# Normalization pairs: the meeting of two half sums moved from VectorE to ScalarE and GpSimd, and the inner factors of the second Strassen level formed in two pieces

## The chip, the cores and the metric

The kernel runs on one core of a Trainium2 chip. A time is the device time of one execution in microseconds (us), and where several runs are given their median is used. A core has TensorE (PE, the matrix engine), VectorE (DVE), ScalarE (ACT), GpSimd (POOL) and the queues that start transfers (DMA); each engine works through its own list of instructions in order, and semaphores make one wait for another. A profiled execution gives start and length of every instruction; its span is the time from the first to the last of them.

## The reference, cut to what matters

```python
batch, n_heads, seq, head_dim = (8, 12, 448, 64)

def rmsnorm(x, g):
    rms = np.sqrt(np.mean(x * x, axis=-1, keepdims=True) + 1e-06)
    return x / rms * g
q_n, k_n = (rmsnorm(q, g_q), rmsnorm(k, g_k))
scores = scale * np.matmul(q_n, k_n.transpose(0, 1, 3, 2))
attn = softmax(scores)
attn_out = np.matmul(attn, v)            # (8, 12, 448, 64) -> x of (8*448, 768)

h = x @ w_in                             # 3584 x 768 x 2048
g = h - np.tanh(h)
out = g @ w_out                          # 3584 x 2048 x 768
```

(The softmax is written out in the reference, with the maximum subtracted; its line is shortened here.) So there are 96 heads of attention with a normalization of every row of q and k, and then a two-layer network over 3584 tokens. The two weights come as float64.

## The kernel before

**Pairs and slots.** The heads are taken in pairs: eight batches of six pairs make 48 steps `s`. The attention of step `s` and the preparation of the following steps are spread over one slot; between the parts of a slot, `run(ns)` lets the network's matmuls of an earlier batch go on for a given amount of work. The network is a generator (`mlp`) which yields the estimated time of each matmul. So nothing is scheduled on the chip: the order of each engine's list is written out by the Python program, in the order in which the slot and the generator call the instructions.

**A slot.** `slot(s)` (from step 12 on) begins with the scores of the next step's last chunk of keys (the `p_last` tiles), and then with `visit`, a run of 128 small matmuls that takes the values of step `s` and the scores of step `s + 1` together. The scores use three PSUM banks in turn; ScalarE's exponentials (line 570) release them. After the visit come fourteen work points, with a share of the network's matmuls ahead of each. Among them are: the sums of the exponentials for step `s + 1` on VectorE (lines 595, 601, 608, then 705 and 712), ScalarE's gathering copies (720), VectorE's scaling and transposes of step `s + 2` (528, 538, 542), ScalarE's squares for step `s + 3` (499), and the normalization of `s + 3`.

**The norm of a pair.** From step 15 on q and k of a pair lie "by blocks": partitions hold four groups of 32 (two heads, two halves of the 64 elements), so a row's sum of squares is in two halves on two groups of partitions. `norm_blocks` (line 506) reduces each half into `rr_mine` (128 x 28). `meet_blocks` (514, 515) adds, group by group, the own half and the partner's into `rr_other`, and scales it and adds the epsilon. `power_blocks` (521) raises it to the power -1/2 on GpSimd, at the start of the next slot. `scale_blocks` (528) multiplies q and k by it.

**The network.** Its products are done by a fast scheme with seven products for a 2 x 2 split, in the order 1, 5, 6, 2, 3, 7, 4 (`ORDER`), with sums of blocks ahead of them. For the first layer (`hidden`, matmuls on line 831) and for the second layer of batches 0 and 1 there is one level. From batch 2 on, two batches form a pair, and their second layer (`project_pair`, matmuls on line 1082) has two levels: seven outer products over (batch, half), each with seven inner products. Two outer products run after the first batch's hidden layer and five after the second's. `outer_sum` (1032, VectorE) forms the outer sums in place; `inner_sum` (1040, GpSimd) forms the four sums `u` of an outer product, each of 128 x 896, in four rotating buffers. Of the inner products, 5, 6, 7 and 4 read the sums 0, 1, 2 and 3. The three `mm` PSUM banks go round: product 3 is added on top of product 5's bank once VectorE has read product 5 (line 1089), and 2 and 7 likewise on top of 1 and 6. The activation of the hidden layer is ScalarE's tanh (878) and a subtraction on GpSimd or VectorE (879), with two `th` buffers; a third tanh waits until the first subtraction has released its buffer. GpSimd also makes the first-level sums of the attention's output (787).

Of the kernel before, what the change touches and what calls it, by code (L numbers as in the profile page):

```python
# [13 lines left out]
ALU = mybir.AluOpType  # L14
# [130 lines left out]
def bounded_path(tc, ctx, q, k, v, moe_w_in, moe_w_out, out, g_col, ident, ones, half_ones, neg_half, early):  # L145
# [17 lines left out]
    nc = tc.nc  # L163
    B, H, S, D = q.shape
# [17 lines left out]
    BL = 32  # L182
# [252 lines left out]
    normed, turned, probs, sums, whole, xT, tt = {}, {}, {}, {}, {}, {}, {}  # L435
# [73 lines left out]
    def meet_blocks(s):  # L509

        mine, other = normed["rr", s]
        for g in range(P // BL):
            own, met = slice(g * BL, (g + 1) * BL), slice((g ^ 1) * BL, ((g ^ 1) + 1) * BL)
            nc.vector.tensor_tensor(out=other[own], in0=mine[own], in1=mine[met], op=ALU.add)  # L514
        nc.vector.tensor_scalar(out=other, in0=other, scalar1=1.0 / D, scalar2=1e-6, op0=ALU.mult, op1=ALU.add)  # L515
        normed["rr", s] = other

    def power_blocks(s):

        mine = normed["rr", s]  # L520
        nc.gpsimd.tensor_tensor(  # L521
            out=mine, in0=mine, in1=neg_half[:, :1].to_broadcast([P, 2 * NJ]), op=ALU.pow
        )
# [26 lines left out]
    def scores(s, c, apart=False):  # L550

        rr, kT, qT = turned[s]
        n = S if c < KF else HS
        name, bufs = ("p", 2) if c < 2 else ("p_full", 1) if c < KF else ("p_last", 2)
        if c == 1:
            p = probs[s, 1] = probs[s, 0]
        else:
            p = probs[s, c] = pp.tile([P, 2, 2 if c < 2 else 1, n], F32, name=name, bufs=bufs)
        tiles = [sc_bank() for _ in range(2)]

        def score(h, i):
            at, first = (i * BL, 0) if c < KF else (i * BL % KR, i * BL // KR * n)
            r = slice(h * D, (h + 1) * D)
            nc.tensor.matmul(  # L564
                tiles[h][i * BL : (i + 1) * BL, :n], lhsT=kT[r, c * P + at : c * P + at + BL],
                rhs=qT[r, first : first + n], start=True, stop=True,
            )

        def exp(h):
            nc.scalar.activation(  # L570
                p[:, h, c if c < 2 else 0, :], tiles[h][:, :n], AF.Exp,
                scale=1.0 if rr is None else rr[:, 0, 2 * c + h : 2 * c + h + 1],
            )

        if apart:
            return [(lambda i, h=h: score(h, i), lambda h=h: exp(h)) for h in range(2)]
        for i in range(P // BL):
            for h in range(2):
                score(h, i)
        for h in range(2):  # L580
            exp(h)
# [28 lines left out]
    def last_values(s, av):  # L610

        v_nat, p = loaded["v", s], probs[s, KF]
        for n in range(2):
            keys, at = slice(n * KR, (n + 1) * KR), n * HS if s >= FOLDED else 0
            for m in range(2):
                for h in range(2):
                    r = (2 * m + h) * BL
                    nc.tensor.matmul(  # L618
                        av[n][r : r + BL, at : at + HS], lhsT=v_nat[keys, h, KF, m * BL : (m + 1) * BL],
                        rhs=p[keys, h, 0], start=(s < FOLDED), stop=False, skip_group_check=(s >= FOLDED),  # L620
                    )
# [54 lines left out]
    def totals(s, dn):  # L676

        parts = [t[:, h, n * HS : (n + 1) * HS] for t in sums.get(s, ()) for n in range(2) for h in range(2)]
        parts = [(parts, [ones[:, :BL]] * 2)] if parts else []
        if not sums.pop(s):  # L680
            for p in full(s):
                parts.append(
                    ([p[:, h, n * HS : (n + 1) * HS] for n in range(2) for h in range(2)], [ones[:, :BL]] * 2)
                )
            last = probs[s, KF]
            parts.append(([last[:, h, 0] for _ in range(2) for h in range(2)], [half_ones[:, n] for n in range(2)]))
        for i, (moving, by) in enumerate(parts):
            for n in range(2):
                for h in range(2):
                    r = (2 * n + h) * BL  # L690
                    nc.tensor.matmul(
                        dn[r : r + BL, :HS], lhsT=by[n], rhs=moving[2 * n + h],
                        start=(i == 0), stop=(i == len(parts) - 1),
                    )
        rs = whole[s] = sp.tile([P, HS], F32, name="rs")
        nc.vector.reciprocal(rs, dn[:, :HS])
# [34 lines left out]
    def widen_sums(s):  # L731

        total = whole[s]
        wide = whole[s] = late["blocks"].tile([2 * BL, NJ, BL], F32, name="sum_w")
        nc.scalar.copy(out=wide, in_=total[:, :, None].to_broadcast([2 * BL, NJ, BL]))

    def turn_sums(s):

        wide = whole[s]
        rs = whole[s] = late["blocks"].tile([2 * BL, S], F32, name="rs_T")  # L740
        nc.vector.transpose(out=rs, in_=wide.rearrange("p j k -> p (j k)"))
# [273 lines left out]
    KB = HF // 2  # L1015

    def rows(p, f, n, cols):
        which, half = HOME[p]
        return late["pair_g"][which][:, half * HF + f : half * HF + f + n, cols]
# [14 lines left out]
    def inner_sum(p, i):  # L1034

        us = late["us"]
        x11, x12, x21, x22 = (rows(p, f, KB, cols) for f in (0, KB) for cols in (slice(0, HS), slice(HS, S)))
        u = us[p, i] = late["pair"].tile([P, KB, HS], F32, name="u", bufs=4)
        a, z = ((x12, x11), (x22, us.get((p, 0))), (x22, x12), (x21, us.get((p, 1))))[i]
        nc.gpsimd.tensor_tensor(out=u, in0=a, in1=z, op=ALU.subtract)  # L1040

    def beside_hidden(b, j, p):

# [258 lines left out]
    def gap_ns(s):  # L1302

        if s < 2 * NP:
            return H_NS / 12 if s % NP < 3 else 4 * S / ENGINE_NS * CD * CF / 12
        if s < 3 * NP:
            return (H_NS + O_NS + AHEAD_NS) / (4 * NP)
        n = (s - 3 * NP) % (2 * NP)
        return (H_NS / 16, OUTER_NS * SOON / 8, H_NS / 16, OUTER_NS * (len(OUTER) - SOON) / 8)[(n > 3) + (n > 5) + (n > 9)]

    def has(s):
        return 0 <= s < NS
# [69 lines left out]
    def slot(s):  # L1382

        gap = gap_ns(s)
        av = av_banks
        if has(s + 1):
            scores(s + 1, KF)
        if s < FOLDED:
            last_values(s, av)
            totals(s, sc_bank())  # L1390
            divide(s, values(s, av))
            for c in range(KF):
                scores(s + 1, c)
        else:
            visit(s, av)
        if has(s + 2):
            load(s + 2, "v")
        rows, ahead, following = has(s + 2), has(s + 3), has(s + 1)
        folded = following and s + 1 >= FOLDED
        first = s + 3 == TURNED  # L1400
        scaled = rows and not first
        if scaled:
            power_blocks(s + 2)
        work = (
            (
                (following, lambda: add(s + 1, False)), (first, lambda: turn(s + 2, sc_bank(), sc_bank())),
                (ahead and not first, lambda: load_blocks(s + 3)),
            ),
            (
                (following, lambda: add_third(s + 1)), (first, lambda: load_blocks(s + 3)),  # L1410
                (True, lambda: x_sums_later(s, 0)),
            ),
            ((following, lambda: add_last(s + 1)),),
            ((folded, lambda: fold(s + 1)),),
            ((folded, lambda: fold_rest(s + 1)), (True, lambda: x_sums_later(s, 1))),
            ((scaled, lambda: scale_blocks(s + 2)),),
            ((scaled, lambda: turn_blocks(s + 2, 0)),),
            ((folded, lambda: gather(s + 1, 0)), (scaled, lambda: turn_blocks(s + 2, 1))),
            ((folded, lambda: gather(s + 1, 1)), (ahead, lambda: square_blocks(s + 3))),
            ((folded, lambda: spread_sums(s + 1)), (True, lambda: x_sums_later(s, 2))),  # L1420
            ((ahead, lambda: norm_blocks(s + 3)),),
            ((folded, lambda: widen_sums(s + 1)), (ahead, lambda: meet_blocks(s + 3))),
            ((folded, lambda: turn_sums(s + 1)),),
            (),
        )
        for point in work:
            run(4 * gap / (len(work) + 1))
            for wanted, fn in point:
                if wanted:
                    fn()  # L1430
        run(4 * gap / (len(work) + 1))
# [358 lines left out]
```

## Time and profile before

| | |
|---|---|
| time, median of 3 runs | 1406.79 us (1406.57 to 1408.85) |
| profiled execution: time, span | 1407.51 us, 1405.4 us |
| PE busy | 1341.7 us, 95% of the span |
| DVE busy | 1077.7 us, 77% |
| POOL busy | 727.2 us, 52% |
| ACT busy | 523.3 us, 37% |
| mean granted TensorE clock | 0.985 |
| DVE meets: 132 additions (514) and 33 scalings (515) | 80.2 and 17.9 us busy |
| POOL powers (521), 33 | 166.8 us |
| POOL inner sums (1040), 84 | 195.8 us in all |

In a group's row the columns are: line, engine, operation, tiles written and read, shapes, count, then busy time and mean length of one in ns, then the idle time of the engine just before these instructions, with what ended most of it. In a list of waits the numbers are the total, how often, and the longest, in us. In a timeline the columns are start (us from the span's start), length, engine, line, operation, tiles and count, with idle time before it in brackets.

### The profile page before, as it was taken

How to read it: one execution, taken by the hardware profiler on the slowest of the kernel's cores; microseconds unless marked ns; L12 is line 12 of the kernel's file. 1: busy time of each engine (PE TensorE's matmuls, PEld its weight loads, DVE VectorE, ACT ScalarE, POOL GpSimd, SP SyncE). 2: the span in 40 equal slices, each digit the busy share in tenths (PEclk: the TensorE clock that was granted, in tenths of full speed). 3: DMA queues.
4: the chain of work that ended last, by engine and by line, in shares of the span. 5: the costliest groups of instructions: out<-in, count | busy, mean ns of one | idle time of the engine just before them, and what ended most of it. 6: DMA issues, size and time to landing. Idle time of an engine off the chain costs nothing.

```text
span 1405.4 us, 29010 instructions
## 1 busy us (share of the span) xinstructions
PE 1341.7 (95%) x11336; PEld 1048.9 (75%) x11336; DVE 1077.7 (77%) x1558; ACT 523.3 (37%) x1194; POOL 727.2 (52%) x409
## 2 busy tenths in 40 slices
PE   7988999999999998999999999999999999899996
PEld 3467854488889885788768787678876788689884
DVE  4999989669857888789988688879997688533563
ACT  7856554343332533343321434253511244311100
POOL 4756666156762439335784336733597234712661
PEclk9999999999999999999999999999999999999998
DMA  7879889889998665475545866375644775355544
GB/s 173 187 208 252 267 240 243 254 230 329 328 267 238 162 178 124 92 200 156 130 128 143 190 173 166 89 173 155 165 120 126 154 199 151 102 155 171 168 150 80
DMA packets 371686, 253.52 MB, mean 180 GB/s; under 512 B 282196, under 2 KB 310228, under 8 KB 371540
## 3 DMA queue, kind: packets, MB, share of 16 engines
q1 hardware_dynamic: 371536, 251.57, 66.4%
q8 instruction: 92, 1.51, 0.4%
q14 instruction: 54, 0.44, 0.1%
q10 hardware_dynamic: 4, 0.00, 0.0%
HBM read 205.23 MB, written 46.27 MB: 179 GB/s over the span
## 4 chain that ended last, share of the span: by engine, by line
PE 71%; DVE 17%; DMA 4%; issue 3%; SPq 2%; ACT 1%; POOL 1%; ACTq 0%; DVEq 0%; POOLq 0%
PE mm L831 34%; PE mm L1082 17%; PE sc L564 8%; PE mm L1246 5%; PE sc L630 5%; DVE rr_other L514 2%; DVE rows L608 2%; DMA w_f<-w_in 1%; DMA gT<-in_moe_w_in_dram 1%; DVE acc L1089 1%; PE sc L668 1%; DVE g L1032 1%; DVE xT L756 1%; PE sc L618 1%; DVE rows L601 1%
## 5 line engine op out<-in xcount | busy, mean ns | idle before, releaser
L831 PE MATMUL mm<-xT,w_f 128*128 128x224 f32 x1296 | 264.3, 353 | 1.7 <-DVE s L902 1.7
L831 PEld LDWEIGHTS mm<-xT,w_f 128*128 128x128 f32 x1296 | 244.4, 190 | 8.2 <-issue 4.3
L564 PE MATMUL sc<-qT,kT 64*32 64x448 f32 (+1 forms) x3072 | 217.8, 500 | 4.3 <-ACT p_last L570 3.1
L831 PE MATMUL mm<-tt,w_f 128*128 128x224 f32 x1044 | 213.3, 355 | 0.4
L521 POOL TENSOR_TENSOR rr_other<-rr_other,neg_half 128x28 f32<-128x28 f32 x33 | 166.8, 5056 | 83.8 <-DVE rr_other L515 83.2
L831 PEld LDWEIGHTS mm<-tt,w_f 128*128 128x128 f32 x1044 | 195.2, 190 | 17.7 <-issue 15.4
L879 POOL TENSOR_TENSOR gT<-s,th 128x448 f32<-128x448 f32 x60 | 73.3, 1236 | 201.3 <-ACT th L878 199.4
L1082 PE MATMUL mm<-gT,w_f 128*128 128x224 f32 (+1 forms) x480 | 138.6, 443 | 13.7 <-DVE acc L1089 12.6
L1082 PE MATMUL mm<-u,w_f 128*128 128x224 f32 x672 | 139.8, 360 | 1.3 <-DVE acc L1089 1.3
L1082 PEld LDWEIGHTS mm<-u,w_f 128*128 128x128 f32 x672 | 130.0, 195 | 8.6 <-issue 4.5
L1082 PEld LDWEIGHTS mm<-gT,w_f 128*128 128x128 f32 x480 | 92.9, 196 | 53.7 <-issue 36.2
L564 PEld LDWEIGHTS sc<-qT,kT 64*32 64x32 f32 x3072 | 73.1, 106 | 76.3 <-issue 45.6
L879 POOL TENSOR_TENSOR g<-s,th 128x448 f32<-128x448 f32 x36 | 43.3, 1216 | 165.8 <-ACT th L878 150.4
L630 PE MATMUL sc<-p,v_nat 64*32 64x448 f32 x1120 | 119.4, 537 | 0.0
L1082 PE MATMUL mm<-g,w_f 128*128 128x224 f32 (+1 forms) x360 | 104.2, 443 | 11.5 <-DVE s L1089 6.9
L1082 PEld LDWEIGHTS mm<-g,w_f 128*128 128x128 f32 x360 | 70.4, 197 | 39.8 <-issue 26.0
L720 ACT COPY sum_g<-sum 32x14 f32<-32x14 f32 x280 | 56.3, 201 | 112.9 <-DVE sum L712 107.2
L752 DVE TENSOR_TENSOR xT<-xT,sc 128x448 f32<-128x448 f32 x32 | 19.7, 617 | 101.2 <-PE sc L564 58.5
L570 ACT ACTIVATE p<-sc 128x448 f32<-128x448 f32 x132 | 72.0, 546 | 40.4 <-PE sc L564 35.9
L514 DVE TENSOR_TENSOR rr_other<-rr_mine 32x28 f32<-32x28 f32 x132 | 80.2, 607 | 3.8
L1246 PE MATMUL mm<-gT,w_out 128*128 128x448 f32 x192 | 74.3, 542 | 0.0
L878 ACT ACTIVATE th<-s 128x448 f32<-128x448 f32 x96 | 53.1, 571 | 54.4 <-DVE s L910 16.7
(187 smaller groups left out, 2429.0 us busy)
## 6 DMA issues: line engine op xcount, KB each, us to landing
w_f<-w_in SPq DMA_DIRECT2D x196, 384.0 KB, 3.5
w_f<-w_inner SPq DMA_DIRECT2D x63, 512.0 KB, 3.6
w_f<-w_out SPq DMA_DIRECT2D x42, 512.0 KB, 3.9
w_raw<-in_moe_w_out_dram SPq DMA_DIRECT2D x16, 768.0 KB, 5.3
w_in<-w_out SPq DMA_DIRECT2D x21, 384.0 KB, 5.5
qk_nat<-in_q_dram SPq DMA_DIRECT2D x132, 56.0 KB, 2.6
qk_nat<-in_k_dram SPq DMA_DIRECT2D x132, 56.0 KB, 2.5
g<-w_out SPq DMA_DIRECT2D x14, 512.0 KB, 5.4
```

What stands on the lines that cost most here:

```text
L514: nc.vector.tensor_tensor(out=other[own], in0=mine[own], in1=mine[met], op=ALU.add)
L521: nc.gpsimd.tensor_tensor(out=mine, in0=mine, in1=neg_half[:, :1].to_broadcast([P, 2 * NJ]), op=ALU.pow)
L564: nc.tensor.matmul(tiles[h][i * BL : (i + 1) * BL, :n], lhsT=kT[r, c * P + at : c * P + at + BL], rhs=qT[r, first : first + n], start=True ...
L570: nc.scalar.activation(p[:, h, c if c < 2 else 0, :], tiles[h][:, :n], AF.Exp, scale=1.0 if rr is None else rr[:, 0, 2 * c + h : 2 * c + h ...
L608: nc.vector.tensor_tensor(out=part, in0=part, in1=last[n * KR : (n + 1) * KR], op=ALU.add)
L630: nc.tensor.matmul(av[g][i * BL : (i + 1) * BL, :S], lhsT=v_nat[keys, h, c, m * BL : (m + 1) * BL], rhs=p[keys, h], start=first, stop=True ...
L720: nc.scalar.copy(out=acc[h * BL : (h + 1) * BL, g], in_=part[g * BL : (g + 1) * BL, h * NJ : (h + 1) * NJ])
L831: nc.tensor.matmul(bank[:, f * HS : (f + 1) * HS], lhsT=w[:, c * width + f, :], rhs=moving[p](c), start=(first and f == 0 and c == 0), sto ...
L878: nc.scalar.activation(th, h, AF.Tanh, bias=0.0, scale=1.0)
L879: eng.tensor_tensor(out=g[:, rows, cols], in0=h, in1=th, op=ALU.subtract)
L1082: nc.tensor.matmul(bank[:, :n], lhsT=w(i), rhs=mv, start=(first and i == 0), stop=(i == len(moving) - 1), skip_group_check=not first,)
L1246: nc.tensor.matmul(bank[:, :S], lhsT=w_out_row(f, n // HC)[:, n % HC * P : (n % HC + 1) * P], rhs=g[:, f, :], start=(f == 0), stop=(f == C ...
```

## The change

Two edits. First, ScalarE copies the partner's half (`rr_mine` of the neighbouring group of 32 partitions) into `rr_other`, four copies of 32 x 28, one work point later than VectorE's additions were; GpSimd then adds `rr_other` to `rr_mine`, scales and adds the epsilon, and raises to the power, all at the start of the next slot. VectorE no longer takes part. Second, every inner sum `u` is made by two GpSimd instructions of 128 x 448 in place of one of 128 x 896.

```diff
         mine, other = normed["rr", s]
         for g in range(P // BL):
-            own, met = slice(g * BL, (g + 1) * BL), slice((g ^ 1) * BL, ((g ^ 1) + 1) * BL)
-            nc.vector.tensor_tensor(out=other[own], in0=mine[own], in1=mine[met], op=ALU.add)
-        nc.vector.tensor_scalar(out=other, in0=other, scalar1=1.0 / D, scalar2=1e-6, op0=ALU.mult, op1=ALU.add)
-        normed["rr", s] = other
+            nc.scalar.copy(out=other[g * BL : (g + 1) * BL], in_=mine[(g ^ 1) * BL : ((g ^ 1) + 1) * BL])
 
     def power_blocks(s):
 
-        mine = normed["rr", s]
+        mine, other = normed["rr", s]
+        nc.gpsimd.tensor_tensor(out=mine, in0=mine, in1=other, op=ALU.add)
+        nc.gpsimd.tensor_scalar(out=mine, in0=mine, scalar1=1.0 / D, scalar2=1e-6, op0=ALU.mult, op1=ALU.add)
+        normed["rr", s] = mine
         nc.gpsimd.tensor_tensor(
             out=mine, in0=mine, in1=neg_half[:, :1].to_broadcast([P, 2 * NJ]), op=ALU.pow
         )
@@
         a, z = ((x12, x11), (x22, us.get((p, 0))), (x22, x12), (x21, us.get((p, 1))))[i]
-        nc.gpsimd.tensor_tensor(out=u, in0=a, in1=z, op=ALU.subtract)
+        for half in (slice(0, KB // 2), slice(KB // 2, KB)):
+            nc.gpsimd.tensor_tensor(out=u[:, half], in0=a[:, half], in1=z[:, half], op=ALU.subtract)
@@
             ((ahead, lambda: norm_blocks(s + 3)),),
-            ((folded, lambda: widen_sums(s + 1)), (ahead, lambda: meet_blocks(s + 3))),
-            ((folded, lambda: turn_sums(s + 1)),),
+            ((folded, lambda: widen_sums(s + 1)),),
+            ((folded, lambda: turn_sums(s + 1)), (ahead, lambda: meet_blocks(s + 3))),
             (),
```

## The prediction

> **What bounds the kernel now.** The first part of the page and the shares of the chain came first:
>
> ```profile
> PE 1341.7 (95%) x11336; PEld 1048.9 (75%) x11336; DVE 1077.7 (77%) x1558; ACT 523.3 (37%) x1194; POOL 727.2 (52%) x409
> PE 71%; DVE 17%; DMA 4%; issue 3%; SPq 2%; ACT 1%; POOL 1%; ACTq 0%; DVEq 0%; POOLq 0%
> ```
>
> PE sets the time and is idle for 1405.4 - 1341.7 = 63.7 us. Removing VectorE work pays only where PE idles for VectorE, so next came the list of PE's waits, with the groups that the change touches:
>
> ```profile
> PE mm L1082 <- DVE acc L1089: 18.6, 10, 2.7
> PE mm L1082 <- DVE s L1089: 8.0, 4, 3.5
> L514 DVE TENSOR_TENSOR rr_other<-rr_mine 32x28 f32<-32x28 f32 x132 | 80.2, 607 | 3.8
> L720 ACT COPY sum_g<-sum 32x14 f32<-32x14 f32 x280 | 56.3, 201 | 112.9 <-DVE sum L712 107.2
> ```
>
> 26.6 us of idle, 14 waits, all in the two-level second layer, where product 3, 7 or the block behind product 4 needs a bank that VectorE has not read yet. The timelines around the first such wait (VectorE, GpSimd, TensorE) say why it is late:
>
> ```profile
> 529.52 7.33 DVE L514 TENSOR_TENSOR rr_other<-rr_mine 32x28 f32<-32x28 f32 x4
> 536.89 1.05 DVE L515 TENSOR_SCALAR rr_other<-rr_other 128x28 f32<-128x28 f32 x1
> ...
> 530.59 2.12 POOL L1040 TENSOR_TENSOR u<-gT,u 128x896 f32<-128x896 f32 x1
> 532.66 2.12 POOL L1040 TENSOR_TENSOR u<-gT 128x896 f32<-128x896 f32 x1
> 534.73 2.08 POOL L1040 TENSOR_TENSOR u<-gT,u 128x896 f32<-128x896 f32 x1
> ...
> 536.36 1.68 PE L1082 MATMUL mm<-gT,w_f 128*128 128x224 f32 x8
> 540.77 3.33 PE L1082 MATMUL mm<-gT,w_f 128*128 128x224 f32 x8 [2.73 <-DVE acc L1089]
> ```
>
> A meet addition (median 182 ns on line 514) takes 2.05 us when an inner sum is in flight: each waits for one GpSimd instruction to end. Five instructions worth 0.9 us hold VectorE from 529.5 to 537.9, and the read of product 5 comes at 540.32. And behind the gap eight matmuls take 3.33 us, not 1.68: the granted clock was 0.50 in 540.6 to 543.9. I find eight such stretches of 3.41 us behind the waits of this stage. At full use each costs 3.41 x 0.5 = 1.7 us more.
>
> [...] The trace has the 3.41 us stretches, but gaps of 2.2 us bring them; the one of 2.06 us at 884.00 did not. [...]
>
> **The change part by part.** *VectorE loses* 132 additions and 33 scalings, 80.2 + 17.9 = 98 us busy. Its order is otherwise the same. *GpSimd gains* an addition and a scaling of 128 x 28 in front of each power. No row shows them; the subtraction takes 1.13 us at 448 elements (line 879) and 2.07 at 896, so about 0.19 + 2.1 ns x 28 = 0.25 us each, an estimate; bounds 0.1 and 0.65 (the 224-element form of line 787). I take 0.5 us a slot, 17 us in all. *Halved sums:* 2 x 1.13 = 2.26 for 2.07, 0.2 us each, 84 x 0.2 = 17 us of GpSimd. It cuts a VectorE wait from up to 2.05 to up to 1.1 us, and each half has its own wait on PE, so a product can begin 1.1 us ahead of the second half. *ScalarE gains* four copies at a pitch of 0.225 us (line 720: 201 ns), 0.9 us a slot, now in front of the next slot's `p_last`.
>
> *Gain, stage by stage.* (1) Waits at 538.03 (2.73), 547.12 (2.22) and in the second pair at 874.88 (2.63), 884.00 (2.06). Without the meets VectorE is free at 529.5 and waits for ScalarE's xT (534.8, 535.2 with the copies). Line 752 takes 0.6, the two of 756 up to 1.15 each beside half sums, so product 5 is read at 538.1, where PE needs it at 538.03: some 0.1 is left. The chain behind it (595, 601, two of 608, 705) then falls under the power, which does not block VectorE (756, 595 and 601 had their usual 0.6 and 1.1 us beside it), so 608 takes 0.6 and not 2.4, and the block's bank is read at 543.4 for a need at 543.0: 0.4 is left. Saved 2.6 + 1.8 and 2.5 + 1.7 = 8.6, and three half-clock stretches, 5.1.
> (2) At 721.20 and 1056.29 (3.44, 3.46) the meets stand directly in front of the read that PE wants:
>
> ```profile
> 718.92 3.40 DVE L514 TENSOR_TENSOR rr_other<-rr_mine 32x28 f32<-32x28 f32 x4
> 722.35 1.94 DVE L515 TENSOR_SCALAR rr_other<-rr_other 128x28 f32<-128x28 f32 x1
> 724.20 0.68 DVE L1089 TENSOR_TENSOR s<-mm,s 128x224 f32<-128x224 f32 x2
> ```
>
> Both go whole, with their stretches: 6.9 + 3.4 = 10.3.
> (3) At 683.73 and 1018.81 (2.3 each) the wait goes too, but GpSimd is late next:
>
> ```profile
> 682.29 6.09 POOL L521 TENSOR_TENSOR rr_other<-rr_other,neg_half 128x28 f32<-128x28 f32 x1
> 688.35 2.07 POOL L1040 TENSOR_TENSOR u<-g,u 128x896 f32<-128x896 f32 x1
> ...
> 687.99 4.54 PE L1082 MATMUL mm<-u,w_f 128*128 128x224 f32 x16
> ```
>
> Product 4 (the second eight, from 690.85) reads the sum that ends at 690.42. That sum stands behind the power, and now behind two halved sums (0.4) and the two new instructions (0.5). PE would arrive about 687.5 and wait to about 690. I take 0.8 saved each, 1.6, instead of 4.0 each.
> (4) 1209 to 1219, where there are no meets any more (gaps 0.32, 1.08, 2.65): 595 and 601 take 2.6 us beside whole sums; halves save about 1.7 of the gaps, and the stretch stays.
> (5) 642.96 and 978.20 (0.9, 0.8): a 608 of 2.4 us beside a sum; 1.5 saved.
> Sum 8.6 + 5.1 + 10.3 + 1.6 + 1.7 + 1.5 = 28.8.
>
> *Loss: ScalarE in front of p_last.* ScalarE before the visit at 506.86:
>
> ```profile
> 507.47 0.55 ACT L735 COPY sum_w<-sum_all 64x448 f32<-64x448 f32 x1
> 508.37 0.58 ACT L878 ACTIVATE th<-s 128x448 f32<-128x448 f32 x1 [0.36 <-POOL gT L879]
> 508.86 0.51 ACT L898 COPY s<-mm 128x448 f32<-128x448 f32 x1
> 509.27 0.61 ACT L570 ACTIVATE p_last<-sc 128x224 f32<-128x224 f32 x2
> ```
>
> Visits last 5.43 us where `p_last` starts up to 1.3 us after their start, and 6.37 where it starts 2.41 after: what is beyond 1.47 us is lost, since the second wave of scores needs the bank. Already 10 us go so. The copies come behind `sum_w` (the reduction 506 has ended at 507.75): 508.03 to 508.93. 0.36 of it falls into the wait for GpSimd, so the third tanh, the copy 898 and `p_last` come 0.57 later. I did this for all 33 slots: 9 lose about 0.58 (5.2), 6 whose `p_last` is now at 1.13 to 1.19 lose 0.22 to 0.29 (1.5), five others 0.5 in all, 13 nothing, as ScalarE idles there. Sum 7.2; 1.3 of it lies in the slots of (3) and vanishes in the wait for GpSimd: 5.9.
>
> Net -28.8 + 5.9 = -22.9. The profiled execution took 1407.51 (span 1405.4 and 2.1 around it), 0.7 over the median, so 1384.6 for it and 1384 as median. The halved sums' and small instructions' 34 us of GpSimd cost nothing elsewhere, as GpSimd is half idle and the sums of the other products are ready 4 to 20 us ahead; where that cover fails is (3).
>
> **Rivals.** *GpSimd takes the place everywhere.* VectorE's chain re-forms behind half sums (756, 595, 601 at 1.1 us of wait each) and the power, pushed back, no longer covers 608. Then half of (1) is left, 6.9, with (2) 10.3 and (5) 1.5, less 7.2: -11.5, 1395. For it: GpSimd works without a break from 682 to 724. *All of it.* Copies fit into ScalarE's pauses, the half sums let product 4 begin in time, and the gaps of (4) and their stretch go: 28.8 + 6.4 + 4 - 1 = -38, 1369. *Slower: the copies hold up every visit.* If `p_last` slips by the whole 0.9 us in all 33 slots, 29.7 us are lost; the eleven visits that stall already would idle about 2 us, and two half-clock stretches add 3.4. Against 28.8 of gain: +4, 1411. It decides from 28.8/33 = 0.87 us a slot. Against it: in 13 slots ScalarE waits for PE anyway. *The halves do nothing,* since two back-to-back halves keep VectorE out as one does: (4), (5) and a third of (1) go, about 1391; between the cases.
>
> **How the numbers follow.** Forecast, with its own range 1376 to 1392: 0.50. GpSimd in its place or halves without effect, 1391 to 1401: 0.22. All of it: 0.12. Slower: 0.13. About no change (the gaps move on): 0.03. Cutting half of the lowest and most of the slower case leaves 1369 to 1404. A measurement of this kernel tells 0.2% (2.8 us) from no change; the chances are 0.84 faster, 0.03 within, 0.13 slower.
>
> **What would show it.** After: PE idle about 45 us, its waits for line 1089 under 8 us, at most four half-clock stretches after 500 us, new waits of the second layer for `u` of 2 to 3 us near 685 and 1015; 168 half sums of 1.1 to 1.3 us; `p_last` 0.5 us later in the hidden stage, its visits up to 7.0 us. It is wrong if visits of 5.43 us become rare, if the new GpSimd instructions take over 0.65 us, or if reads of product 5 stay late.

## The result, and the profile after

The changed kernel takes 1390.59 us, the median of four runs (1390.16 to 1391.89); the kernel before, run beside it, 1407.47. The ratio is 0.9882 (95% interval 0.987 to 0.9895): 16.9 us less. The span of the profiled execution fell from 1405.4 to 1388.4 us. The forecast was 1384 with a range of 1376 to 1392, so the gain is 6 us smaller than the 22.9 worked out.

The first part of the page after, and the shares of its chain of waits:

```profile
PE 1335.9 (96%) x11336; PEld 1046.3 (75%) x11336; DVE 963.2 (69%) x1393; ACT 550.9 (40%) x1326; POOL 766.1 (55%) x559
PE 75%; DVE 9%; DMA 4%; ACT 4%; POOL 3%; SPq 3%; issue 2%; ACTq 0%; DVEq 0%; POOLq 0%
```

VectorE's share of the chain falls from 17% to 9%, and ScalarE's and GpSimd's grow from 1% each to 4 and 3. PE is idle for 1388.4 - 1335.9 = 52.5 us, 11.2 less than before; the other 5.8 us come from its own busy time, which goes with three stretches at half clock behind 500 us instead of eight (the one at the very end, which both have, apart). The list of PE's waits shows who took VectorE's place (lines below 1040 are the same in both kernels, those after it are one higher now):

```profile
PE mm L1083 <- POOL u L1041: 6.9, 2, 3.5
PE sc L564 <- ACT p_last L570: 6.3, 12, 1.0
PE mm L1083 <- DVE acc L1090: 5.2, 7, 2.6
```

Late reads by VectorE, 26.6 us in 14 waits before, are down to 5.2 in 7. In front stand two waits that did not exist, for an inner sum of GpSimd, and twelve in which the scores of a visit wait for ScalarE's `p_last` (before, three of 3.1 us in all). What the new instructions take, from the one-line views of ScalarE's copies and GpSimd's addition (count, then least, median and longest in ns):

```profile
L513 ACT COPY rr_other<-rr_mine x132: 209/213/216, 301.6 to 1165.6; 32x28 f32<-32x28 f32 x132
L518 POOL TENSOR_TENSOR rr_mine<-rr_mine,rr_other x33: 237/243/1092, 304.7 to 1167.5; 128x28 f32<-128x28 f32 x33
```

A copy takes what the forecast took from line 720, and the addition 0.24 us where nothing holds it up, against an estimate of 0.25; six of the 33 were held up, the longest to 1.09 us.

Both kernels issue the same 11336 matmuls in the same order. So I compare the start of the k-th matmul in both traces and read off how much each stage of the forecast gained or lost (times of the kernel before; us; negative is a gain):

| stage | forecast | measured |
|---|---|---|
| (1) 528 to 566 and 865 to 895 | -13.7 | -12.1 |
| (2) 715 to 740 and 1050 to 1075 | -10.3 | -10.6 |
| (3) 673 to 715 and 1008 to 1050 | -1.6 | +5.6 |
| (4) 1195 to 1225 | -1.7 | -2.2 |
| the rest: visits, (5) | +4.4 | +2.4 |
| sum | -22.9 | -16.9 |

One row differs: (3). The others are off by 2 us at most.

**Where it went as worked out.** VectorE's timeline in stage (1):

```profile
535.71 2.50 DVE L756 TENSOR_TENSOR xT<-xT,rs_T 64x448 f32<-64x448 f32 x2
538.23 0.39 DVE L1090 TENSOR_TENSOR acc<-mm,s 128x224 f32<-128x224 f32 x1
...
541.52 1.27 DVE L608 TENSOR_TENSOR rows<-rows,p_last 64x448 f32<-64x448 f32 x2
...
543.86 0.35 DVE L1090 TENSOR_TENSOR acc<-mm,acc 128x224 f32<-128x224 f32 x1
```

The reads come at 538.23 and 543.86, where 538.1 and 543.4 were forecast. The gaps of 2.73 and 2.22 us shrink to 0.42 and 0.41. Line 608 lies under the power, and two of them take 1.27 us instead of up to 2.4 each.

**Where it did not.** GpSimd's timeline in the first half of stage (3), before the change and after it, and below them PE's after:

```profile
676.90 2.13 POOL L1040 TENSOR_TENSOR u<-g,u 128x896 f32<-128x896 f32 x1
...
680.09 2.08 POOL L1040 TENSOR_TENSOR u<-g 128x896 f32<-128x896 f32 x1
```

```profile
670.39 3.10 POOL L1041 TENSOR_TENSOR u<-g,u 128x448 f32<-128x448 f32 x2
...
674.54 2.61 POOL L1041 TENSOR_TENSOR u<-g 128x448 f32<-128x448 f32 x2
677.11 0.62 POOL L518 TENSOR_TENSOR rr_mine<-rr_mine,rr_other 128x28 f32<-128x28 f32 x1
677.82 0.21 POOL L519 TENSOR_SCALAR rr_mine<-rr_mine 128x28 f32<-128x28 f32 x1
678.12 5.60 POOL L521 TENSOR_TENSOR rr_mine<-rr_mine,neg_half 128x28 f32<-128x28 f32 x1
683.69 2.21 POOL L1041 TENSOR_TENSOR u<-g,u 128x448 f32<-128x448 f32 x2
```

```profile
679.73 1.68 PE L1083 MATMUL mm<-u,w_f 128*128 128x224 f32 x8
684.86 3.36 PE L1083 MATMUL mm<-u,w_f 128*128 128x224 f32 x8 [3.46 <-POOL u L1041]
```

PE is done with product 7 at 681.40 and stands for 3.46 us, until the first half of product 4's sum is ready at 684.8. Then eight matmuls take 3.36 us instead of 1.68: the granted clock is 0.50 from 684.9 to 690.4. The same happens in the second pair (3.46 us of wait, half clock from 1014.7 to 1018.2).

I count from the end of the second subtraction 879 (676.82 before, 670.43 after), which starts GpSimd's work here in both kernels. Before, the power ended 11.6 us later and product 4 began 14.0 us later. After, the power ends 13.3 us later and product 4 begins 14.4 us later, although its first half is enough now. The second pair gives the same 14.0 and 14.4.

### The profile page after: what moved, and what is told of

It reads as the page before. It is cut to its first block, busy times and chain, and to the rows that moved or that the text cites. A ratio compares the mean times of both kernels' runs of the same rounds, so it can differ in the third digit from the quotient of the medians.

```text
span 1388.4 us, 29145 instructions
## 1 busy us (share of the span) xinstructions
PE 1335.9 (96%) x11336; PEld 1046.3 (75%) x11336; DVE 963.2 (69%) x1393; ACT 550.9 (40%) x1326; POOL 766.1 (55%) x559
## 3 DMA queue, kind: packets, MB, share of 16 engines
q8 instruction: 92, 1.51, 0.4%
## 4 chain that ended last, share of the span: by engine, by line
PE 75%; DVE 9%; DMA 4%; ACT 4%; POOL 3%; SPq 3%; issue 2%; ACTq 0%; DVEq 0%; POOLq 0%
PE mm L831 33%; PE mm L1083 22%; PE sc L564 8%; PE mm L1247 5%; PE sc L630 4%; DMA w_f<-w_in 2%; DVE xT L756 1%; PE sc L668 1%; DMA w_raw<-in_moe_w_in_dram 1%; POOL u L1041 1%; DVE rows L608 1%; ACT th L878 1%; PE sc L618 1%; SPq L125 1%; SPq L287 1%
## 5 line engine op out<-in xcount | busy, mean ns | idle before, releaser
L564 PE MATMUL sc<-qT,kT 64*32 64x448 f32 (+1 forms) x3072 | 220.6, 500 | 7.5 <-ACT p_last L570 6.3
L521 POOL TENSOR_TENSOR rr_mine<-rr_mine,neg_half 128x28 f32<-128x28 f32 x33 | 163.8, 4963 | 2.7
L1083 PE MATMUL mm<-gT,w_f 128*128 128x224 f32 (+1 forms) x480 | 133.0, 429 | 5.2 <-DVE acc L1090 5.0
L630 PE MATMUL sc<-p,v_nat 64*32 64x448 f32 x1120 | 122.5, 537 | 0.0
L1041 POOL TENSOR_TENSOR u<-gT 128x448 f32<-128x448 f32 x48 | 65.5, 1385 | 15.6 <-PE mm L1083 15.5
L878 ACT ACTIVATE th<-mm 128x448 f32<-128x448 f32 x32 | 17.4, 543 | 141.2 <-PE mm L831 134.2
```

The lines of the kernel that those rows point to most:

```text
L521: nc.gpsimd.tensor_tensor(out=mine, in0=mine, in1=neg_half[:, :1].to_broadcast([P, 2 * NJ]), op=ALU.pow)
L564: nc.tensor.matmul(tiles[h][i * BL : (i + 1) * BL, :n], lhsT=kT[r, c * P + at : c * P + at + BL], rhs=qT[r, first : first + n], start=True ...
L630: nc.tensor.matmul(av[g][i * BL : (i + 1) * BL, :S], lhsT=v_nat[keys, h, c, m * BL : (m + 1) * BL], rhs=p[keys, h], start=first, stop=True ...
L878: nc.scalar.activation(th, h, AF.Tanh, bias=0.0, scale=1.0)
L1041: nc.gpsimd.tensor_tensor(out=u[:, half], in0=a[:, half], in1=z[:, half], op=ALU.subtract)
L1083: nc.tensor.matmul(bank[:, :n], lhsT=w(i), rhs=mv, start=(first and i == 0), stop=(i == len(moving) - 1), skip_group_check=not first,)
```

## The experiments

Each ran beside the kernel before on the same chip; ratios have their 95% interval. The table splits the change of each run's profiled execution against that of the kernel before, in us, by the stages above, and adds what all visits took beyond 5.43 us each (10.6 before). The visits' loss is contained in the other columns, mostly in the rest. Each row is one execution: those of e5 and e7 are the fastest of their runs (3.9 and 2.8 us below the median), and the number of half-clock stretches ahead of 130 us, one to three where before and after have two, moves the rest by 1.7 us either way.

| run | (1) | (2) | (3) | (4) | rest | sum | visits |
|---|---|---|---|---|---|---|---|
| both edits (after) | -12.1 | -10.6 | +5.6 | -2.2 | +2.4 | -16.9 | 17.3 |
| e1, meet edit alone | -11.9 | -8.8 | +3.7 | +1.3 | +1.7 | -13.9 | 18.5 |
| e2, halves alone | -11.0 | -8.7 | -1.0 | -0.5 | -1.6 | -22.8 | 10.2 |
| e4, no copies, no addition | -12.1 | -10.6 | +0.7 | -2.2 | -4.4 | -28.5 | 10.8 |
| e7, copies twice | -11.0 | -10.6 | -0.1 | -2.2 | +17.9 | -6.1 | 39.4 |
| e3, power later | -12.1 | -10.6 | -1.7 | -0.7 | +2.8 | -22.3 | 18.1 |
| e6, halves alone, power later | -11.0 | -4.9 | -0.1 | -2.2 | -1.6 | -19.8 | 9.3 |
| e5, copies behind the visit | -8.9 | -10.6 | -2.9 | -0.5 | -5.1 | -28.0 | 10.6 |
| e8, same, power sooner | -11.7 | -10.6 | -1.7 | -0.4 | -3.6 | -28.0 | 9.5 |
| e9, quarters | -10.8 | -10.6 | +9.2 | -4.5 | +6.8 | -9.9 | 21.6 |

### Which edit brings the gain: e1 and e2

e1 is the changed kernel with whole inner sums:

```diff
-        for half in (slice(0, KB // 2), slice(KB // 2, KB)):
-            nc.gpsimd.tensor_tensor(out=u[:, half], in0=a[:, half], in1=z[:, half], op=ALU.subtract)
+        nc.gpsimd.tensor_tensor(out=u, in0=a, in1=z, op=ALU.subtract)
```

> The changed kernel with whole inner sums (the first edit alone). Theory (an account by stages: the reads that stood behind the meets, the relief by half sums, the copies in front of p_last, GpSimd's chain in front of product 4): 721 and 1056 gain 10.5, the visits lose 6.6, the sum behind the power costs 5 in the stages of 683 and 1018, and at 538 and 875 the two of line 756 wait 2.05 us each, so only some 5 are gained: about -4, 1403. Rival (taking 98 us off VectorE is the whole gain and the halves do nothing): 1390.

Measured: 1393.51 us beside 1406.14, ratio 0.9908 (0.9891 to 0.9924), near the rival's number and far from mine: stage (1) gains 11.9 us where I expected 5. (The rival's reason, that the halves do nothing, falls with e2.) VectorE's and GpSimd's timelines in stage (1) show why the halves matter so little there once the meets are gone:

```profile
534.72 3.15 DVE L756 TENSOR_TENSOR xT<-xT,rs_T 64x448 f32<-64x448 f32 x2
537.89 0.39 DVE L1089 TENSOR_TENSOR acc<-mm,s 128x224 f32<-128x224 f32 x1
```

```profile
533.83 2.09 POOL L1040 TENSOR_TENSOR u<-gT,u 128x896 f32<-128x896 f32 x1
535.87 1.51 POOL L879 TENSOR_TENSOR gT<-s,th 128x448 f32<-128x448 f32 x1
```

The two of line 756 take 3.15 us here and 2.50 beside halves. Only the first finds a whole sum in its way, and that one ends 1.2 us later; the second waits for a subtraction of 448 elements, where the forecast had a wait of 2.05 us for each. (The whole run is 1 us ahead at this point.) PE's gap here is 1.07 us instead of 0.42, and the one behind it 0.22 instead of 0.41. Neither brings a half-clock stretch, which is why stage (1) still gains 11.9 us. Stage (3) loses 3.7 us here too, without any halves: so much of its loss belongs to the meet edit.

e2 is the kernel before with the second edit only:

```diff
-        nc.gpsimd.tensor_tensor(out=u, in0=a, in1=z, op=ALU.subtract)
+        for half in (slice(0, KB // 2), slice(KB // 2, KB)):
+            nc.gpsimd.tensor_tensor(out=u[:, half], in0=a[:, half], in1=z[:, half], op=ALU.subtract)
```

> The kernel before with halved inner sums (the second edit alone). Theory: a meet addition waits 1.1 in place of 2.05, so 538/547 and 875/884 gain about 10, 721/1056 about 7.6, 1209 and the hidden stage 3; the sum in front of product 4 costs about 4; no loss in the visits: about -16, 1391, as much as both edits together. Rival (the halves do nothing, since back-to-back halves keep VectorE out as a whole does): 1405 to 1408.

Measured: 1384.73 us beside the same 1406.14, ratio 0.9843 (0.9827 to 0.9859). The halves alone beat both edits together; the intervals do not overlap. VectorE's meet in stage (1) and PE's waits in this run:

```profile
529.15 4.46 DVE L514 TENSOR_TENSOR rr_other<-rr_mine 32x28 f32<-32x28 f32 x4
```

```profile
PE mm L1083 <- DVE acc L1090: 10.7, 8, 2.6
PE mm L1083 <- POOL u L1041: 2.2, 4, 0.9
```

An addition of the meet that had to wait for an inner sum took 2.05 us before; now it waits for a half and takes 1.1, so four take 4.46 us instead of 7.33. VectorE then reads product 5 at 538.84, still late, but PE waits only 1.62 us for it, and no half-clock stretch follows. And in stage (3) VectorE, still at its meet, has only short instructions beside GpSimd's sums: the two before the power take 2.2 us each, and the power ends 11.1 us after the second subtraction (13.3 with both edits).

The gains are not added: 12.6 us (meets) and 21.4 (halves) become 16.9. Both take away the same lateness in (1) and (2), 20.7 and 19.7 us of it, and 22.7 together. By the table, the meet edit beside the halves brings 3.0 us there and 1.7 in (4), and loses 6.6 in (3) and 4.0 in the rest: a net loss of 5.9 us. (The 1.7 us in (4) are one half-clock stretch; the last section shows behind what idle time they came.)

### What the copies cost: e4 and e7

e4 leaves the meeting out of the changed kernel: no copies, no addition, and the scaling with twice the own half.

```diff
-            nc.scalar.copy(out=other[g * BL : (g + 1) * BL], in_=mine[(g ^ 1) * BL : ((g ^ 1) + 1) * BL])
+            pass
...
-        nc.gpsimd.tensor_tensor(out=mine, in0=mine, in1=other, op=ALU.add)
-        nc.gpsimd.tensor_scalar(out=mine, in0=mine, scalar1=1.0 / D, scalar2=1e-6, op0=ALU.mult, op1=ALU.add)
+        nc.gpsimd.tensor_scalar(out=mine, in0=mine, scalar1=2.0 / D, scalar2=1e-6, op0=ALU.mult, op1=ALU.add)
```

> The changed kernel without ScalarE's copies and GpSimd's addition: the norm is taken from a row's own half alone, times two; the rest of the work is there. Theory (the copies delay p_last by about 0.57 us): visits are back at about 10.6 us beyond 5.43 in sum instead of 17.3, so about 6.6 less, and GpSimd's chain is 0.3 us shorter: 1383 to 1384. Rival (the visits are longer for another reason, as GpSimd's later subtractions): 1389 to 1391.

Measured: 1381.89 us, ratio 0.9829 (0.9812 to 0.9845), 1 us under the theory's range and far from the rival. The visits fall back to 10.8 us beyond 5.43 each in sum, from 17.3. In stage (3) the power ends 12.1 us after the second subtraction, and PE's two waits for the sum are 2.3 us each instead of 3.46.

e7 makes each copy twice:

```diff
-            nc.scalar.copy(out=other[g * BL : (g + 1) * BL], in_=mine[(g ^ 1) * BL : ((g ^ 1) + 1) * BL])
+            for _ in range(2):
+                nc.scalar.copy(out=other[g * BL : (g + 1) * BL], in_=mine[(g ^ 1) * BL : ((g ^ 1) + 1) * BL])
```

> The changed kernel with each of ScalarE's copies made twice (eight a slot, the same values). Theory (whatever ScalarE does there beyond its pause of 0.36 us delays p_last by its whole length, and beyond 1.47 us each microsecond is lost): 0.9 more in some 18 to 20 slots, two of them hidden behind the wait for GpSimd: +14 to +17, 1405 to 1408, visits about 33 us beyond 5.43 in sum. Rival (ScalarE is half idle and takes it in): under 1395.

Measured: 1403.92 us beside 1408.34, ratio 0.9976 (0.9967 to 0.9984), 13.3 us above the changed kernel, a little less than the 14 to 17 expected, although the visits lose 39.4 us instead of 33. ScalarE's timeline before the visit at 506 in the changed kernel, and then in this one (one line lower):

```profile
507.58 0.91 ACT L513 COPY rr_other<-rr_mine 32x28 f32<-32x28 f32 x4
...
509.41 0.61 ACT L570 ACTIVATE p_last<-sc 128x224 f32<-128x224 f32 x2
```

```profile
508.37 1.89 ACT L514 COPY rr_other<-rr_mine 32x28 f32<-32x28 f32 x8
...
511.18 0.61 ACT L571 ACTIVATE p_last<-sc 128x224 f32<-128x224 f32 x2
```

Four copies take 0.91 us, eight 1.89, and `p_last` follows behind both. In the changed kernel it starts 2.95 us after the start of the visit (2.41 before), and the visit takes 6.91 us (6.37): half a microsecond of slip, half a microsecond of loss, as the rule of the forecast has it. Doubled, the copies cost 22 us more in the visits, but only 10.8 between the two traces (13.3 between the medians): PE comes so late to stage (3) that its waits for the sum shrink to 2.0 us and the half clock behind them is gone, so that (3) is 5.7 us shorter although its own visits are longer.

### What makes stage (3) late: e3

The power, with its addition and scaling, goes one work point later, so that GpSimd makes product 4's sum first:

```diff
-        if scaled:
-            power_blocks(s + 2)
         work = (
             (
+                (scaled, lambda: power_blocks(s + 2)),
                 (following, lambda: add(s + 1, False)), (first, lambda: turn(s + 2, sc_bank(), sc_bank())),
```

> The changed kernel with GpSimd's addition, scaling and power moved one work point later in the slot, so that the inner sum for product 4 of the third outer product is ahead of them. Theory: the two waits of 3.46 us for this sum go (6.9), and with them the half-clock stretches behind them (3.4 and 1.7): 1378 to 1380. Rival (TensorE would wait there anyway, for VectorE or for the weights): over 1387. The visits stay as they are, at about 17 us beyond 5.43 each in sum.

Measured: 1385.58 us, again beside 1406.14, ratio 0.9853 (0.9837 to 0.9869). GpSimd's timeline in stage (3), and PE's wait for its sums:

```profile
677.47 3.45 POOL L1041 TENSOR_TENSOR u<-g,u 128x448 f32<-128x448 f32 x2
...
685.66 5.16 POOL L521 TENSOR_TENSOR rr_mine<-rr_mine,neg_half 128x28 f32<-128x28 f32 x1
```

```profile
PE mm L1083 <- POOL u L1041: 2.4, 6, 0.5
```

The two waits of 3.46 us become six of at most 0.5, and the half-clock stretches in (3) are gone. Stage (3) goes from +5.6 to -1.7, 7.3 us better. So it is shown that the power in front of the sum makes (3) late. The time is some 6 us above what I expected. By the starts of the matmuls, stage (3) gains 11.3 us around product 4, about the 12.0 expected, and loses 4.0 again further on, as the next sums stand behind the power now; the six waits are 2.4 of these. In (4) a half-clock stretch came back (+1.5), and the rest loses 0.4 more.

e6 does the same with the halves alone:

```diff
-        if scaled:
-            power_blocks(s + 2)
...
+                (scaled, lambda: power_blocks(s + 2)),
```

> The kernel before with halved inner sums (the second edit alone), and GpSimd's power one work point later, ahead of which the sum for product 4 now goes. Theory: beside the halves alone (1384.7) the waits of 0.9 and 0.2 us for that sum go in both pairs, and later sums wait by some 0.5 twice, as they did with the changed kernel: 1383 to 1385, no difference that counts. Rival (the power's place is worth 5 us whatever else is there, as it was with both edits): 1380.

Measured: 1388.11 us beside 1408.34, ratio 0.9871 (0.9845 to 0.9897): no gain over e2, against both expectations. There the wait is not GpSimd's. The sum that now comes first runs beside VectorE's 756, which takes 2.37 us for two instead of 1.26, and VectorE's read of product 5 comes later: PE waits 2.9 us for it in each pair where it waited 1.8. In the second pair it also waits 2.38 us instead of 0.65 near 1040. Half-clock stretches follow both waits of the second pair, and none follows that of the first. Moving the power helps only where the wait is for what stands behind the power.

### A version that beats both: e5 and e8

In e5 the copies are called right behind the visit, where `p_last` is already done, and the power moves to the second work point:

```diff
         if scaled:
-            power_blocks(s + 2)
+            meet_blocks(s + 2)
...
+                (scaled, lambda: power_blocks(s + 2)),
                 (True, lambda: x_sums_later(s, 0)),
...
-            ((folded, lambda: turn_sums(s + 1)), (ahead, lambda: meet_blocks(s + 3))),
+            ((folded, lambda: turn_sums(s + 1)),),
```

> The changed kernel with ScalarE's four copies moved behind the next visit's exponentials, and GpSimd's addition, scaling and power moved two work points later, behind them. Theory (the copies cost the visits 6.6, the sum behind the power some 5): visits back at 10 to 11 us beyond 5.43 in sum, no wait of over 1 us for the sum of product 4, VectorE's meets still gone: 1377 to 1380. Rival (VectorE's scaling of q and k comes to wait for the later power, and the visits gain little): 1386 or more.

Measured: 1382.46 us (1378.58 to 1385.55), ratio 0.9834 (0.9803 to 0.9864). The visits are back at 10.6. But in (1) 3 us are lost: a sum goes ahead of the power there now, VectorE's 608 runs beside it (2.09 us for two instead of 1.27), and PE waits 1.83 us in each pair for the read behind it. So e8 takes the first work point:

```diff
         if scaled:
-            power_blocks(s + 2)
+            meet_blocks(s + 2)
         work = (
             (
+                (scaled, lambda: power_blocks(s + 2)),
                 (following, lambda: add(s + 1, False)), (first, lambda: turn(s + 2, sc_bank(), sc_bank())),
...
-            ((folded, lambda: turn_sums(s + 1)), (ahead, lambda: meet_blocks(s + 3))),
+            ((folded, lambda: turn_sums(s + 1)),),
```

> As the copies behind the visit, but GpSimd's addition, scaling and power one work point later than in the changed kernel, not two. Theory: the power again covers the additions of line 608 at 543 and 866, where the later power left 1.83 us twice, while the sums for product 4 stay ahead of it: 1.4 less twice, 1378 to 1380. Rival (the chain of waits has no such place left, and the time is that of the copies behind the visit): 1382 to 1383.

Measured: 1379.27 us beside 1407.28, ratio 0.9796 (0.978 to 0.9812), the lowest of all. ScalarE's timeline and the list of PE's waits:

```profile
509.74 0.61 ACT L570 ACTIVATE p_last<-sc 128x224 f32<-128x224 f32 x2
...
514.92 0.92 ACT L513 COPY rr_other<-rr_mine 32x28 f32<-32x28 f32 x4
```

```profile
PE sc L564 <- ACT p_last L570: 2.6, 4, 1.5
PE mm L1083 <- POOL u L1041: 2.4, 6, 0.5
```

The copies keep their 0.92 us, but they come behind `p_last` now, and the visits are at 9.5. Its time cannot be told from e5's (the intervals overlap, and both traces are 28.0 us shorter than that of before), so whether the first or the second work point is the better place for the power stays open; the 2.8 us that e8 wins back in (1) are seen in the trace alone. It can be told from those of the changed kernel and of the halves alone.

### Smaller pieces: e9

```diff
-        for half in (slice(0, KB // 2), slice(KB // 2, KB)):
+        for half in (slice(c, c + 1) for c in range(KB)):
```

> The changed kernel with each inner sum in four pieces of 128 x 224. Theory (a VectorE instruction waits for one GpSimd instruction, and the sum for product 4 is late by GpSimd's own work): VectorE's waits at 538, 1195 and 1201 shrink by 0.3 to 1 us each, but a piece costs 0.65, so a sum takes 2.6 and the waits at 681 and 1010 stay or grow by some 0.5: 1388 to 1392, no clear gain. Rival (what VectorE waits for beside the sums still decides): 1383 or less.

Measured: 1397.07 us beside 1407.28 (20 executions from 1394.2 to 1407.5, of which six lie above 1403), ratio 0.9946 (0.9928 to 0.9964), slower than I expected and 6.5 us slower than halves. A quarter takes 0.66 us in the median and up to 1.57, four of them 2.6 us for a sum that took 2.07 whole. The two waits for a sum in (3) grow to 4.4 and 5.6 us, with two half-clock stretches behind each. In (4), where VectorE's reads are what is late, quarters do help (-4.5); in (1), where I expected the same, a wait of 1.26 us stays.

## Why the prediction was right, and where its size was off

**What bounds the kernel** held: where VectorE's reads came in time, PE gained. Stages (1) and (2) were worked out as 24.0 us and gave 22.7.

**Step (3)** failed. "I take 0.8 saved each" was to be a start of product 4 at 13.2 us after the second subtraction; it was 14.4, 1.2 later in each pair, 2.4 in all. The terms: the two sums ahead of the power took 3.10 and 2.61 us (2.13 and 2.08 before), 1.5 more where "two halved sums (0.4)" stood. VectorE, no longer at its meet, has its own instructions beside them:

```profile
669.76 1.62 DVE L1032 TENSOR_TENSOR gT<-g,gT 128x896 f32<-128x896 f32 x1
...
675.48 2.15 DVE L756 TENSOR_TENSOR xT<-xT,rs_T 64x448 f32<-64x448 f32 x2
```

The same two sums, left whole, in e1:

```profile
669.42 2.83 POOL L1040 TENSOR_TENSOR u<-g,u 128x896 f32<-128x896 f32 x1
...
673.31 2.10 POOL L1040 TENSOR_TENSOR u<-g 128x896 f32<-128x896 f32 x1
```

So 0.7 of the 1.5 come with the meet edit (1032 is now in front of the first sum, whose halves take 2.00 and 1.14 us) and 0.8 with the cut, 0.4 of which were foreseen; the second half of the second sum lets a 756 go first (1.51 us where the first half takes 1.13). Addition and scaling took 1.0 us to the start of the power where 0.5 stood; the power itself gave 0.5 back. The halves did let product 4 start 1.1 us ahead of the whole sum, as written. The rest is the clock: the step foretold a wait of some 2.5 us in front of product 4, and left out that every wait over 2.2 us in the two-level second layer of the trace of before has a half-clock stretch behind it. Three came, two in a row in the first pair. The first of these began 1.2 us before PE did, so they cost about 2.8 us there and 1.7 in the second pair, 4.5 in all. Together 6.9 us, against 7.2 measured as the miss. That product 4's sum is late because it stands behind the power is shown by e3; that the loss needs the meet edit, by e1 (+3.7 without halves) and e2 (-1.0 with halves alone). That VectorE's instructions hold up the sums is read from the timelines, and no run moved them alone.

**ScalarE in front of p_last** held: 7.2 us foretold, 17.3 - 10.6 = 6.7 measured, taken away by e4 and by e8's order, raised by e7.

**(4)** came near by luck. "The stretch stays" was wrong, it went; and the gaps shrank from 4.05 to 3.39 us, 0.7 instead of 1.7. Behind the same gap of 2.65 us e2, e3, e5 and e8 have a stretch, and e4, e6 and e7 have none.

**The halved sums** cost GpSimd 32 us (195.8 to 228.2) where 17 stood. Outside (3) PE never waited for a sum, as said.

**The rivals.** "GpSimd takes the place everywhere" named the right engine, but GpSimd takes it in one stage only. The measured 1390.6 lies just below the 1391 where this rival and "the halves do nothing" begin, so the time alone does not tell them from the forecast; the stages and e2 do. "Slower: the copies" had a real mechanism, with 6.7 us instead of 29.7; doubled, it nearly eats the gain (e7). "The halves do nothing" fell outright: alone they give 21.4 us. None of the cases had them as the stronger edit, or the meet edit as a loss beside them: I costed both against the kernel before, and not one against the other.

**What would show it**: waits for the reads under 8 us (5.2), at most four half-clock stretches after 500 us (3), waits for `u` near 685 and 1015 (there, 3.46 us instead of 2 to 3), and visits of about 7.0 us in the hidden stage all came (the longest, 7.3, is as long as before). PE's idle time was to be 45 us and is 52.5. A half sum was to take 1.1 to 1.3 us: the median is 1.14, but the mean 1.36, as 60 of the 168 took longer. Of the signs of being wrong one came in part: four additions on GpSimd took over 0.65 us.

## What to carry to other kernels

When two edits aim at the same late instruction, work out each in the presence of the other: here one alone was better than both. An engine that is relieved comes earlier to its next work and can hold up another engine there, as VectorE seems to do in stage (3) (GpSimd's two halved sums ahead of the power take 5.7 us, and 4.5 in e2, where VectorE is still at its meet), so look at what that engine has to finish just then. Small work moved to an engine that is mostly idle costs what stands behind it in that engine's list; the same four copies cost 6.7 us in front of the release of a bank that PE wants, and nothing that the visits show behind it.

## What the runs showed of the hardware

**In these traces half clock was not decided by the length of a gap alone, but by where it lay.** In (4) the halves alone and the changed kernel have the same two gaps, 0.74 and 2.65 us, and the same work behind them. The clock (the column with 0.50 or 1.00, behind the busy times) of the stretch behind the second gap, in e2 and then in the changed kernel:

```profile
1197.00:1200.20 3.20, 3.20 (x6) 1.51 (x5) 1.84 (x6) 2.03 (x9) 3.20 (x4) 0.50 0.00 0
```

```profile
1204.10:1207.50 3.40, 3.40 (x9) 1.73 (x10) 2.31 (x6) 1.75 (x9) 3.40 (x5) 1.00 0.04 14
```

In each of the eleven traces all half-clock stretches start on one grid of 3.413 us. Counted in the windows of this grid from 130 to 1365 us, PE's idle time told what followed: all 23 windows at full clock in which PE stood 1.99 us or more are followed by one at half clock, and none with 1.92 us or less is. In e2 the gap of 2.65 us lies in one window, in the changed kernel it is cut by a border, into 1.1 and 1.5 us (PE's busy time is the first number behind the comma):

```profile
1193.39:1196.80 3.41, 0.76 (x4) 0.35 (x3) 3.34 (x5) 0.00 (x0) 3.33 (x5) 1.00 0.48 154
```

```profile
1199.07:1202.48 3.41, 2.30 (x13) 1.95 (x11) 3.34 (x3) 0.00 (x0) 3.41 (x3) 1.00 0.28 79
1202.48:1205.89 3.41, 1.88 (x5) 1.06 (x6) 3.27 (x7) 0.82 (x5) 3.33 (x5) 1.00 0.47 145
```

The gap of 2.06 us at 884.00, which brought none, is cut in the same way, into 1.27 and 0.79. A window at half clock was followed by another where PE stood 0.61 us or more in it (four times), and by full clock where it stood 0.48 or less; so a gap of 3.46 us brought two stretches in the first pair, where 1.2 us of it reached into the first of them, and one in the second. A microsecond saved elsewhere shifts the work against the grid, and can so bring or take a stretch in a place that it did not touch; in (4) that is the 1.7 us between e2 (-0.5) and the changed kernel (-2.2).

**VectorE and GpSimd held each other up in both directions.** In the changed kernel a half sum of 1.1 us takes up to 2.05 (2.00 at 670.39, beside VectorE's 1032). A meet addition of 0.18 us takes 2.05 beside a whole sum (before) and at most 1.21 beside a half (e2). So cutting the pieces shortened VectorE's waits, and let GpSimd be held up once more at a cut: in stage (3) the second sum, with two of line 756 beside it, took 2.61 us in halves (the changed kernel) and 2.10 whole (e1).
